# One more VectorE memset among the constants of a decode kernel: two columns of a scratch tensor that nothing reads

## The chip, the cores and the metric

The kernel runs on one core of a Trainium2 chip. A core has five engines that run their own instruction streams and meet at semaphores: TensorE (PE, with its weight loads shown as PEld), VectorE (DVE), ScalarE (ACT), GpSimd (POOL) and SyncE (SP, which here issues nearly all DMAs). The metric is the device time of one execution in microseconds (us); the time before is the median of 3 runs, 192.17 us (192.02 to 192.25).

## The reference

One token is decoded: x is a row of 512. A first block normalizes it, projects it to 32 query heads of 128, attends with 8 key/value heads (each shared by 4 query heads) over 16384 cached positions, and projects back. A second block normalizes again, mixes and goes through an MLP of 1792 with two residual sums.

```
q = (layernorm(x) @ wq)            # 32 heads x 128
scores = q . k_cache / sqrt(128)   # 16384 positions, 8 key heads of 4 queries each
p = softmax(scores)
o = p . v_cache
h = x + o @ wo
out = h + B(layernorm(h))          # B: LN, w1, gelu, shifts, w2, then LN, w3, gelu, w4
```

The caches hold 8 x 16384 x 128 bf16 values each, 33.6 MB for the keys and as much for the values; with the weights that the kernel reads, 79.17 MB come from HBM in one execution. For a single token the shifts of the second block move their one row out of the sequence, so w1 and w2 do not enter, and the kernel does not load them.

## The kernel before, in words

A small class, Program, takes every operation in program order with the keys that it reads and writes, and works out who must wait for whom. When the program is emitted, an operation gets a semaphore increment only if a later one depends on it (`needed`, lines 73 to 85), and each engine's operations are issued in the order in which they were recorded. There is no planner: the order on an engine is the order of the calls.

SyncE first issues three loads: wq (L321, into the buffer that later holds values), and the two halves of the keys of the first pair of heads (L322, L323). ScalarE issues the load of x (L320).

Meanwhile the prologue runs. VectorE fills mean4 and ident_f (L325, L326), GpSimd makes ident_f the identity (L327), VectorE derives quarter (L332, L333). TensorE spreads x over partitions (L335), and `row_sums`, `variance`, `seeds` and `inverse_root` normalize it on VectorE with a few tiny matmuls; the result is the column tensor xn (L341). Then come the constants, which is where the change stands: nscale (L346), zo and zd (L348, L349), reductions of the identity to row32, maskdd, maskgh, rowgh, rowc (L353 to L361) and two copies into zo and zd (L364). At the same time GpSimd zeroes qb and pt (L350, L351). `scr` is a scratch tensor of 128 x 4; ScalarE writes its first column at L347 and its second at L478, only to have the Exp and Gelu tables loaded in time. Its columns 2 and 3 are not used.

When wq has landed, TensorE projects the queries (L375, reads xn and wq), VectorE transposes them (L379) and spreads them into qb (L385).

The main part is a loop over four pairs of key heads. For each half y of a pair's keys, VectorE transposes the half in eight steps (`transpose_keys`, L394, kt from kb), and TensorE multiplies it with the queries (`scores`, L402, 32 matmuls); then SyncE may load the next pair's keys into that half. `softmax` (L413 to L434) follows, `values` (L441) multiplies with the values, `gather` (L452 to L458) collects, and SyncE loads the next values. The second pair's keys (WHOLE) come in one load of both halves.

After the four pairs come wo (L500), the second normalization, w3 (L523), gelu, w4 (L545), the residual sum (L549) and the store of the row (L551). `spin` issues matmuls whose results are not used.

Of the kernel before, what the change touches and what calls it, by code (L numbers as in the profile page):

```python
# [132 lines left out]
def bass_sequential_preLN__gqa_block_cached__mixer_s_mlp__decode_kernel(  # L133
# [13 lines left out]
    with ExitStack() as ctx:  # L147
# [29 lines left out]
        scr = sb("scr", [128, 4], FP32)  # L177
# [62 lines left out]
        def dve(fn, r=(), w=(), bank=()):  # L240
            return P.op("DVE", fn, r, w, bank)

        def act(fn, r=(), w=(), bank=()):
            return P.op("ACT", fn, r, w, bank)
# [99 lines left out]


        dve(lambda e: e.memset(nscale[:, :], -SCALE), w=["nscale"])  # L346
        act(lambda e: e.activation(scr[0:1, 0:1], mean4[0:1, 0:1], ACTF.Exp), r=["mean4"], w=["scr"])  # L347
        dve(lambda e: e.memset(zo[:, :], 0.0), w=["zo"])  # L348
        dve(lambda e: e.memset(zd[:, :], 0.0), w=["zd"])  # L349
# [235 lines left out]
```

## Time and profile before

| what | us |
|---|---|
| median of 3 runs | 192.17 |
| lowest and highest run | 192.02, 192.25 |
| the profiled execution, its own time | 192.12 |
| its span, first to last instruction | 190.4 |
| TensorE matmul busy | 118.2 (62%) |
| VectorE busy | 115.0 (60%), 176 instructions |
| ScalarE busy, GpSimd busy | 9.0, 7.3 |
| HBM read over the span | 79.17 MB, 416 GB/s |
| mean granted TensorE clock | 0.845 |

The page of the profile has the busy time of each engine, the DMA queues, the chain of work that ended last, and groups of instructions. "The chain" is followed back from the last instruction to what released it, and so on; its shares say what the end hung on. In a timeline a row has the start, the duration, engine, line, operation, output <- input with shapes, a count if several were merged, and in brackets how long the engine was idle before it and what ended that. DMA queues of kind "instruction" fetch the engines' code.

### The profile page before, as it was taken

The page shows a single profiled execution, that of the slowest core. Times are in us where ns is not written, and L with a number is a line of the kernel's source. Part 1 is how long each engine was busy: PE and PEld are TensorE (multiplying, and loading weights), DVE is VectorE, ACT ScalarE, POOL GpSimd, SP SyncE. Part 2 cuts the span into 40 slices and gives each one's busy share as a digit, 9 for nine tenths or more (in the row PEclk, how much of TensorE's full clock was granted, in tenths as well). Part 3 has the DMA queues.
Part 4 walks back from the last instruction along what each step waited for, and adds up shares of the span by engine and source line. Part 5 has one row for each costly group of instructions (what it writes and reads, how often), then busy time and mean ns, then how long its engine had stood idle before and what let it go on. Part 6 is the DMA issues. An engine that isn't in the chain of part 4 may idle for free.

```text
span 190.4 us, 1725 instructions
## 1 busy us (share of the span) xinstructions
PE 118.2 (62%) x725; PEld 44.9 (24%) x725; DVE 115.0 (60%) x176; ACT 9.0 (5%) x15; POOL 7.3 (4%) x16
## 2 busy tenths in 40 slices
PE   0129099793083005999449599943739896588673
PEld 0115034221031001422123232212313222233231
DVE  7754697983402008999350999945159897514172
ACT  3000000002000000000110000001000000500011
POOL 7100000000000000000000000000000000000032
PEclk9999859998559655999855789995887999879998
DMA  6999999999999999997999999988999999989991
GB/s 220 441 441 441 441 441 442 441 441 430 441 441 441 441 441 427 441 441 341 441 441 441 530 441 427 416 365 379 434 420 441 468 444 441 427 380 403 443 389 55
DMA packets 2614, 79.26 MB, mean 416 GB/s; under 512 B 304, under 2 KB 432, under 8 KB 560
## 3 DMA queue, kind: packets, MB, share of 16 engines
q1 hardware_dynamic: 2600, 79.17, 97.0%
q8 instruction: 5, 0.08, 0.2%
q14 instruction: 1, 0.01, 0.0%
q10 hardware_dynamic: 8, 0.00, 0.0%
HBM read 79.17 MB, written 0.00 MB: 416 GB/s over the span
## 4 chain that ended last, share of the span: by engine, by line
DMA 60%; DVE 32%; PE 5%; SPq 1%; issue 1%; ACT 1%; ACTq 0%
DMA kb<-in_A_k_cache_dram 46%; DVE kt L394 29%; DMA kb<-in_B_w_dram 14%; PE O_ps L441 3%; DVE pt L428 1%; SPq L221 1%; DVE mx L413 1%; ACT p_sb L424 1%; DVE od L455 1%; PE s_ps L402 1%; PE mn_ps L545 0%; PE mn_ps L418 0%; PE mn_ps L414 0%; DVE od L452 0%; DVE nm L416 0%
## 5 line engine op out<-in xcount | busy, mean ns | idle before, releaser
L402 PE MATMUL s_ps<-kt,qb 128*128 128x512 bf16 x256 | 69.5, 412 | 25.7 <-DVE kt L394 23.0
L394 DVE STREAM_TRANSPOSE kt<-kb 128x1024 int32<-128x1024 int32 x64 | 72.8, 1205 | 18.0 <-DMA kb<-in_A_k_cache_dram 18.0
L402 PEld LDWEIGHTS s_ps<-kt,qb 128*128 128x128 bf16 x256 | 22.9, 103 | 71.3 <-DVE kt L394 46.4
L441 PE MATMUL O_ps<-vb,pt 128*32 128x512 bf16 x256 | 20.1, 484 | 9.8 <-DMA vb<-in_A_v_cache_dram 5.7
L452 DVE TENSOR_SCALAR od<-O_ps,rowc 128x128 f32<-128x128 f32 x4 | 1.4, 351 | 26.2 <-PE O_ps L441 26.2
L441 PEld LDWEIGHTS O_ps<-vb,pt 128*32 128x32 bf16 x256 | 8.4, 119 | 20.7 <-issue 10.9
L428 DVE STREAM_TRANSPOSE pt<-p_sb 64x1024 bf16<-64x1024 bf16 x8 | 9.9, 1239 | 5.4 <-ACT p_sb L424 5.3
L424 ACT ACTIVATE p_sb<-s_ps,bias 128x1024 bf16<-128x1024 f32 x4 | 4.5, 1114 | 156.8 <-DVE nmh L420 156.8
L258 PE MATMUL O_ps<-kt,qb 128*128 128x512 bf16 x31 | 9.3, 443 | 0.0
L413 DVE TENSOR_REDUCE mx<-s_ps 128x1 f32<-128x1024 f32 x4 | 4.9, 1225 | 4.5 <-PE s_ps L402 4.5
L375 PE MATMUL O_ps<-vb,xn 128*64 128x512 bf16 x16 | 3.6, 632 | 5.6 <-DMA vb<-in_A_wq_dram 5.6
L310 POOL TENSOR_SCALAR st<-st 128x1 f32<-128x1 f32 x1 | 0.2, 243 | 177.8 <-DVE st L295 177.8
L430 PE MATMUL A_ps<-acc,zd 128*128 128x1 f32 x8 | 2.1, 337 | 6.3 <-ACT p_sb L424 6.3
L458 PE MATMUL A_ps<-od,zo 128*128 128x128 f32 x8 | 2.0, 326 | 5.5 <-DVE od L455 5.5
L414 PE MATMUL mn_ps<-ident_f,mx 128*1 128x128 f32 x8 | 1.5, 271 | 5.3 <-DVE mx L413 5.3
L455 DVE SCALAR_TENSOR_TENSOR od<-O_ps,rowc,od 128x128 f32<-128x128 f32 x12 | 4.2, 351 | 0.4
L332 DVE CAST ident<-ident_f 4x4 bf16<-4x4 f32 x1 | 3.8, 3847 | 0.6 <-POOL ident_f L327 0.6
L258 PEld LDWEIGHTS O_ps<-kt,qb 128*128 128x128 bf16 x31 | 3.1, 113 | 4.0 <-issue 2.4
L335 PE MATMUL O_ps<-x,quarter 4*128 4x128 bf16 x1 | 0.3, 282 | 5.8 <-DVE quarter L333 5.8
L379 DVE STREAM_TRANSPOSE qcol<-O_ps 128x256 f32<-128x256 f32 x4 | 1.6, 428 | 3.6 <-PE O_ps L375 3.6
L430 PEld LDWEIGHTS A_ps<-acc,zd 128*128 128x128 f32 x8 | 1.8, 280 | 6.6 <-ACT p_sb L424 6.6
L500 PE MATMUL O_ps<-kb,o_b 128*32 128x512 bf16 x32 | 2.1, 381 | 1.7 <-DMA kb<-in_A_wo_dram 1.7
(81 smaller groups left out, 48.1 us busy)
## 6 DMA issues: line engine op xcount, KB each, us to landing
kb<-in_A_k_cache_dram SPq DMA_DIRECT2D x6, 4096.0 KB, 23.2
vb<-in_A_wq_dram SPq DMA_DIRECT2D x1, 4096.0 KB, 12.1
kb<-in_A_wo_dram SPq DMA_DIRECT2D x1, 3072.0 KB, 27.2
kb<-in_B_w_dram SPq DMA_DIRECT2D x1, 1792.0 KB, 24.2
kb<-in_B_w_dram SPq DMA_DIRECT2D x1, 1280.0 KB, 27.0
kb<-in_A_wo_dram SPq DMA_DIRECT2D x1, 1024.0 KB, 29.3
kb<-in_B_w_dram SPq DMA_DIRECT2D x1, 384.0 KB, 27.5
kb<-in_B_w_dram SPq DMA_DIRECT2D x1, 128.0 KB, 27.4
```

The costliest lines, as they stand in the source:

```text
L258: pe(lambda e: e.matmul(O_ps[out][:, :], qb[:, 0, 0, 0:128], kt[:, 0:512], start=True, stop=True), r=["qb", ("kt", 0)], w=[("O", out)], ba ...
L332: dve(lambda e: e.tensor_copy(ident[:, :], ident_f[0:4, 0:4]), r=["ident_f"], w=["ident"])
L375: pe(lambda e, row=row, k=k, g=g, at=at: e.matmul(row[64 * g:64 * g + 64, :], copies(xn[:, k:k + 1], 64), wq_sb[:, at:at + REP * DH], star ...
L394: dve(lambda e, view=view: e.transpose(view(kt), view(kb[y])), r=[("r", y, n) for n in range(RPARTS)], w=[("kt", t)])
L402: pe(lambda e, n=n, c=c: e.matmul(s_ps[:, y, :], qb[:, n, j, QPAD - 4 * c:QW - 4 * c], ktv[:, n // 2, n % 2, :, 8 * c:8 * c + 8, :], start ...
L413: dve(lambda e: e.tensor_reduce(mx[:, :], s_all, AX.X, ALU.max), r=[("s", 0), ("s", 1)], w=["mx"], **both)
L424: act(lambda e: e.activation(p_sb[:, :], s_all, ACTF.Exp, bias=bias[:, 0:1], scale=float(SCALE), accum_out=acc[:, :]), r=[("s", 0), ("s", ...
L428: dve(lambda e, g=g: e.transpose(pt[64 * g:64 * g + 64, :, :, g, :], p_sb[64 * g:64 * g + 64, :]), r=["p"], w=["pt"])
L430: pe(lambda e: e.matmul(A_ps[:, 128:129], zd[:, 96 - 32 * j:224 - 32 * j], acc[:, :], start=(j == 0), stop=(j == PAIRS - 1), skip_group_ch ...
L441: pe(lambda e, q=q, ct=ct, xl=xl, ch=ch: e.matmul(O_ps[j % 2][32 * ct:32 * ct + 32, :], pt[:, xl, ch, :, :].rearrange("p g u -> p (g u)"), ...
L455: dve(lambda e, block=block, c=c: e.scalar_tensor_tensor(od[:, :], block, rowc[:, c:c + 1], od[:, :], ALU.mult, ALU.add), r=[key, "rowc", ...
L500: pe(lambda e, r_=r_, q=q: e.matmul(O_ps[0][32 * q:32 * q + 32, :], copies(o_b[:, r_:r_ + 1], 32), wo_sb[:, r_ * D:(r_ + 1) * D], start=(r ...
```

## The change

One call is added between the memset of nscale and ScalarE's first activation. It writes zeros to columns 2 and 3 of scr on all 128 partitions under a key of its own, "scr2", that no other operation names.

```diff
         dve(lambda e: e.memset(nscale[:, :], -SCALE), w=["nscale"])
+        dve(lambda e: e.memset(scr[:, 2:4], 0.0), w=["scr2"])
         act(lambda e: e.activation(scr[0:1, 0:1], mean4[0:1, 0:1], ACTF.Exp), r=["mean4"], w=["scr"])
         dve(lambda e: e.memset(zo[:, :], 0.0), w=["zo"])
         dve(lambda e: e.memset(zd[:, :], 0.0), w=["zd"])
```

## The prediction

> **What bounds the kernel now.** I read the share of the chain of waits first, then the chain in order of time, then the instructions of the stretch where the change stands, then what the vector engine waits for there, and last the DMA queues. The page's queues (packets, MB, share of the 16 DMA engines' time) and the engines' shares of the chain that ended last:
>
> ```profile
> q1 hardware_dynamic: 2600, 79.17, 97.0%
> q8 instruction: 5, 0.08, 0.2%
> q14 instruction: 1, 0.01, 0.0%
> ...
> DMA 60%; DVE 32%; PE 5%; SPq 1%; issue 1%; ACT 1%; ACTq 0%
> ```
>
> The kernel is bound by its loads: 79.17 MB on one queue whose packets fill 97.0% of the 16 DMA engines' time, and 60% of the chain. VectorE has 32% of the chain, but the chain in order of time says where that share lies:
>
> ```profile
> 1.62 31.52 DMA kb<-in_A_k_cache_dram
> 33.13 0.02 issue
> 33.16 9.14 DVE kt L394 x8
> 42.30 0.02 SPq L101
> 42.32 0.03 issue
> 42.35 29.97 DMA kb<-in_A_k_cache_dram
> 72.32 0.02 issue
> 72.35 18.15 DVE kt L394 x16
> ```
>
> The first 33.13 us of the chain hold no instruction of VectorE at all: the keys' load, issued by 1.62 us, ends that stretch. VectorE enters the chain at 33.16, with the transposes of the second half of the keys. The change stands at about 10.65 us. The timeline of that stretch:
>
> ```profile
> 1.69 3.85 DVE L332 CAST ident<-ident_f 4x4 bf16<-4x4 f32 x1 [0.57 <-POOL ident_f L327]
> ...
> 3.72 1.80 POOL L351 MEMSET pt<- 128x2048 bf16 x1
> ...
> 10.49 0.17 DVE L346 MEMSET nscale<- 1x128 f32 x1
> 10.65 0.24 DVE L348 MEMSET zo<- 128x224 f32 x1
> 10.89 0.24 DVE L349 MEMSET zd<- 128x224 f32 x1
> 11.07 0.23 DVE L353 TENSOR_REDUCE row<-ident_f 128x32 f32<-128x128 f32 x1
> ...
> 12.10 0.18 DVE L364 COPY zd<-maskgh 128x32 f32<-128x32 f32 x1
> ...
> 14.96 0.78 DVE L379 STREAM_TRANSPOSE qcol<-O_ps 128x256 f32<-128x256 f32 x2 [2.68 <-PE O_ps L375]
> ```
>
> The constants run back to back from 10.49 to 12.28; then VectorE stands still for 2.68 us until the query projection delivers. Further on in the same engine's timeline:
>
> ```profile
> 22.62 9.13 DVE L394 STREAM_TRANSPOSE kt<-kb 128x1024 int32<-128x1024 int32 x8 [1.49 <-DMA kb<-in_A_k_cache_dram]
> 33.16 9.13 DVE L394 STREAM_TRANSPOSE kt<-kb 128x1024 int32<-128x1024 int32 x8 [1.41 <-DMA kb<-in_A_k_cache_dram]
> ```
>
> Twice more VectorE is ahead of its data, by 1.49 us and by 1.41 us, before it first matters for the end.
>
> **The change part by part.** It removes nothing and moves nothing in the order of the other engines. It adds one instruction on VectorE, between nscale at L346 and zo at L348, and one instruction to that engine's code.
>
> The instruction's own time. No memset of 128x2 stands in the trace on VectorE. The nearest rows from above are zo and zd, 128x224, 0.24 us each, and 0.24 us from zo's start to zd's; nscale, 1x128, has 0.17 us and 0.16 us to the next start. The nearest row from below is on another engine: the four memsets of 128x1 at the start of GpSimd's timeline begin 0.03 us apart (0.24, 0.27, 0.29, 0.32 us). So the slot is between 0.03 and 0.24 us. I take 0.16, the step from nscale's start, because it is the memset with the fewest elements in a partition on the engine concerned. A gain from the slot itself is excluded: an instruction added in a row that is back to back cannot bring the others forward.
>
> What lies beside it. The constants end at 12.28 + 0.16 = 12.44 us instead of 12.28. The next VectorE instruction starts at 14.96, released by TensorE, so 2.52 of the 2.68 us are left: cost nothing. Does TensorE wait for the constants? The table of waits names the last copy, zd at L364, as what ended 5.6 us of idle weight-load time before L375, and the DMA of wq as what ended 5.6 us of the matmuls' idle time there. L375 reads only xn and the wq buffer in the code, and xn was done by 10.25 + 0.29 = 10.54 us, ahead of the change. So I take the DMA as the releaser: zd is merely the latest event of that engine. Even with the worse reading, zd ended at 12.28 and the weight load began at 12.97, which leaves 0.69 us for a shift of at most 0.24. Nothing that the constants make is wanted early: maskgh first at L420 (45.87 us), rowc at L452 (58.25 us).
>
> If that cover were gone, 0.16 to 0.24 us would go to the projection, then into the 1.49 us that VectorE waits for the first keys at 22.62, and still not to the end. SyncE's next issue after the first three loads is the values at 19.51 us, behind the projection; a delay of 0.24 us there would leave the queue full, since the keys it already holds land only at 33.13.
>
> Semaphores. The helper gives an increment only to an operation on which another depends. Nobody reads or writes the new key afterwards, so the instruction neither waits nor signals, and every other wait keeps its number. Nothing is queued behind a new wait, on any engine. The scratch tensor keeps its size, so no buffer moves. No DMA is added.
>
> The code. VectorE's stream is one instruction longer, so a fetch of code bound to a place in that stream comes one instruction earlier. The page shows six such packets: five on q8 (0.08 MB together) and one on q14 (0.01 MB). Narrow windows of the DMA view place the q14 packet between 30 and 31 us, with 1.9% of 16 engines in 1 us, that is 0.30 us of one engine; a q8 packet between 43 and 45 us has 3.4% of 2 us, that is 1.09 us. If the q14 packet is VectorE's, it moves forward by one transpose, 9.13 / 8 = 1.14 us, within the same wait for the keys. VectorE's eight transposes around it run with no gap that the timeline shows (9.13 us, as in the undisturbed group at 33.16), so today a fetch stalls nothing; I set zero. The two ends: +1.09 us if the move exposes a whole fetch on the chain, and -1.09 us if a fetch that now holds up the last packets of a load on the chain gets out of its way.
>
> The Trainium skill, "Runtime: NRT & Kernel Launch", section "Instruction fetch mechanics", says that code comes in 16 KiB blocks fetched while the current one executes, and that crossing a block's boundary is mostly hidden. By that rule the sum is the same zero. This trace agrees on the hiding, and on the block for q8 (0.08 MB in 5 packets), not for q14, whose packet is 0.01 MB.
>
> The sum. 0.16 us of VectorE, all inside 2.68 us of idle time; +0.00 on the path. The profiled execution has 192.12 us, of which 190.4 is the span and 1.72 lies around it. I expect 192.12 + 0.00, and as the median of the runs shown is 192.17, 0.05 above the profiled one, I give 192.17.
>
> **The rivals.** A measurement of this kernel can tell about 0.2%, 0.38 us, from no change; the three runs shown lie within 0.23 us.
>
> Slower, by a code fetch. The longer stream moves the place where VectorE needs new code to a point on the chain: the transposes at 33.16 to 42.30, 72.35 to 90.50, or those of the two later pairs. Price 0.30 us (the q14 packet) to 1.09 us (a q8 packet), giving 192.47 to 193.26; it decides from 0.38 us on, and only beyond 33.16, since before that 1.41 us of waiting for the keys absorbs it. For it: six fetches do happen, five beside work on which the end depends. Against it: none of VectorE's groups of eight transposes shows a gap, and five of six fetches are on a queue that shows up again and again while TensorE works through its far longer stream (1450 of 1725 instructions).
>
> Slower, by a collision with GpSimd. The 4x4 cast at L332 took 3.85 us where the copy after it took 0.21, and it ended at 5.54 when GpSimd's memset of pt ended (3.72 + 1.80 = 5.52). A small VectorE instruction can thus cost 3.64 us too much. Price of the same for the new memset: 3.64 - 2.68 = 0.96 us late at the projection, taken up by the 1.49 us before the keys, so 192.17 again; it decides only if the delay passes 2.68 + 1.49 = 4.17 us plus 0.38. Against it: GpSimd has no instruction between 5.52 us and its steps of the second normalization after 183 us, so there is nothing to collide with at 10.65. The Trainium skill, "SBUF — State Buffer", calls the port pair that these two engines share an exclusive lock, held for the whole instruction, which fits the cast's 3.85 us; by that rule too the memset is free here.
>
> Faster, by a code fetch out of the way. The fetch that shares the DMA engines with the keys' load ending at 33.13 comes elsewhere, and the load lands earlier. Price 0.30 us for the q14 packet, 191.87, under the bound; with a large one 1.09 us, 191.08. Against it: moved by 1.14 us the packet is still within the same load.
>
> No change because nothing is there: the dead memset is dropped in the build. That ends at 192.17 too.
>
> **How the numbers follow.** No effect (hidden or dropped, the collision included): 0.72. A fetch exposed on the chain: 0.20, of which about 0.16 passes the bound. A fetch out of the way: 0.08; and some 0.04 more on this side is for a shift between two builds of the same work that I can't name, so faster 0.11, same 0.72, slower 0.17. The likeliest case gives 192.17. Its own range is that of the runs shown with 0.1 us around it, 191.9 to 192.4. The range asked for takes in the small form of the faster case (191.87) and over half of the fetch's prices: 191.85 to 192.80; what is left out are the large fetches on either side, about 0.15.
>
> **What would show it.** Right: a memset on scr of about 0.1 to 0.2 us at 10.65, zo at about 10.8, the last constant ending by 12.5; the wait before L379 down from 2.68 to about 2.5 with its start still at 14.96; the keys' landings at 33.13 and 72.32 unmoved; the chain's lines with the same shares. If the q14 packet is VectorE's, it stands near 29.4 instead of 30.5. Wrong: the first group of eight transposes over 9.13 us or a gap inside a group (a fetch), the keys landing other than at 33.13, a start of L375 other than 12.97, or a code packet more than the six.

## The result and the profile after

The change made the kernel faster by a little: 191.75 us median (22 runs, 191.53 to 191.98) against 192.07 us for the kernel before (22 runs beside them, 191.84 to 193.44), a ratio of 0.9978 with a 95% interval of 0.9971 to 0.9986. The time predicted was 192.17 with a range from 191.85, so the median lies 0.10 us below the range, and on the side that had a chance of 0.11.

The first thing to look at is where the 0.32 us are. The profiled execution after has 191.53 us and a span of 190.2, so 1.3 us lie around the span; before it was 192.12 and 190.4, so 1.7. Over all runs that list a span, the medians are:

| | time | span | time less span, median | its range |
|---|---|---|---|---|
| before (31 runs of a later call) | 192.11 | 190.4 | 1.69 | 1.63 to 1.75 |
| after (22 runs) | 191.75 | 190.4 | 1.34 | 1.28 to 1.39 |

The span did not change. What lies around it became 0.35 us shorter, and the two ranges do not touch. So the gain isn't in any work that the page shows. The page after says the same: in its part on the queues and in the chain's shares there is nothing new.

```profile
q1 hardware_dynamic: 2600, 79.17, 97.1%
q8 instruction: 5, 0.08, 0.2%
q14 instruction: 1, 0.01, 0.0%
...
DMA 61%; DVE 31%; PE 4%; issue 1%; SPq 1%; ACT 1%; ACTq 0%
```

The timeline of the stretch with the change (start, duration, engine, line, operation):

```profile
10.50 0.17 DVE L346 MEMSET nscale<- 1x128 f32 x1
10.62 0.06 DVE L347 MEMSET scr<- 128x2 f32 x1
10.67 0.24 DVE L349 MEMSET zo<- 128x224 f32 x1
...
12.12 0.17 DVE L365 COPY zd<-maskgh 128x32 f32<-128x32 f32 x1
...
15.18 0.78 DVE L380 STREAM_TRANSPOSE qcol<-O_ps 128x256 f32<-128x256 f32 x2 [2.88 <-PE O_ps L376]
```

The memset is there and takes 0.06 us. From nscale's start to zo's it is 0.17 us where it was 0.16, and the last constant ends at 12.29 instead of 12.28. All of this lies in front of 2.88 us of idle time. The projection started 0.22 us later because wq landed 0.22 us later in this execution (the run below with the memset late in the program, whose prologue is the old one, has the projection's first weights at 13.14 instead of 12.97 too). The chain in order of time shows how little that matters:

```profile
1.63 31.27 DMA kb<-in_A_k_cache_dram
32.90 0.03 issue
32.92 9.14 DVE kt L395 x8
42.06 0.02 SPq L101
42.08 0.03 issue
42.11 30.19 DMA kb<-in_A_k_cache_dram
72.30 0.02 issue
72.32 18.16 DVE kt L395 x16
```

The second half of the keys landed at 32.90 instead of 33.13, but the second pair's keys landed at 72.30 instead of 72.32: the early gain is lost within one load.

What comes after the span is not on the page, but the trace records every update of a semaphore, with its time. After the last DMA of the kernel a first barrier ends (its last update of semaphore 2 is at 190.70 us before, 190.50 after), then the other semaphores are reset in five rows side by side, read here as one row for each engine, and then semaphore 2 is updated nine times more, in the last barrier: five updates up a row of engines and four back, as the records are read here; they do not name the engines. (The Trainium skill, "Runtime: NRT & Kernel Launch", section "Semaphores 0–2 are reserved", gives semaphore 2 to the sync barrier, which fits this record.) These are the nine in us from the span's start, worked out from the records of both traces:

```
before  191.515 191.550 191.588 191.631 191.655 | 192.123 192.161 192.195 192.242
after   191.293 191.327 191.365 191.409 191.432 | 191.533 191.571 191.605 191.652
```

From one update to the next it is 0.02 to 0.05 us, and at the turn of the row it is 0.10 us after the change, but 0.47 us before it. One engine answered 0.37 us late at the turn in the kernel before. That is nearly all of the 0.40 us by which the time less the span of these two executions differs; the other 0.03 us lie ahead of the barrier. In the barrier that opens the kernel the turn takes 0.11 us in both traces.

### The profile page after: what moved, and what is told of

Same layout as the page of the kernel before. It is cut to its first block, busy times and chain, and to the rows that moved or that the text cites. A ratio compares the mean times of both kernels' runs of the same rounds, so it can differ in the third digit from the quotient of the medians.

```text
span 190.2 us, 1723 instructions
## 1 busy us (share of the span) xinstructions
PE 116.9 (61%) x722; PEld 43.7 (23%) x725; DVE 115.0 (60%) x177; ACT 9.0 (5%) x15; POOL 7.4 (4%) x16
## 4 chain that ended last, share of the span: by engine, by line
DMA 61%; DVE 31%; PE 4%; issue 1%; SPq 1%; ACT 1%; ACTq 0%
DMA kb<-in_A_k_cache_dram 46%; DVE kt L395 28%; DMA kb<-in_B_w_dram 14%; PE O_ps L442 3%; DVE pt L429 1%; SPq L221 1%; DVE mx L414 1%; ACT p_sb L425 1%; DVE od L456 1%; PE s_ps L403 1%; PE mn_ps L546 0%; PE mn_ps L419 0%; PE mn_ps L415 0%; DVE od L453 0%; DVE nm L417 0%
## 5 line engine op out<-in xcount | busy, mean ns | idle before, releaser
L403 PEld LDWEIGHTS s_ps<-kt,qb 128*128 128x128 bf16 x256 | 22.3, 102 | 72.7 <-DVE kt L395 49.4
L376 PEld LDWEIGHTS O_ps<-vb,xn 128*64 128x64 bf16 x16 | 1.5, 168 | 7.1 <-DVE zd L365 5.8
```

Of the source, the lines that this page charges most:

```text
L376: pe(lambda e, row=row, k=k, g=g, at=at: e.matmul(row[64 * g:64 * g + 64, :], copies(xn[:, k:k + 1], 64), wq_sb[:, at:at + REP * DH], star ...
L403: pe(lambda e, n=n, c=c: e.matmul(s_ps[:, y, :], qb[:, n, j, QPAD - 4 * c:QW - 4 * c], ktv[:, n // 2, n % 2, :, 8 * c:8 * c + 8, :], start ...
```

## The experiments

The theory to be tested (A): VectorE is the engine that is late. Somewhere in its stream it has to wait for its code, in the kernel before this falls on its answer in the last barrier, and one instruction more moves it by one. From the run with four more on the theory is more exact: one late step of about 0.35 us at each change from a block of code to the next, 128 or more instructions apart. The rivals: any newly built program gets rid of the delay by luck (B); the gain lies in the span after all (C); the pattern repeats every few instructions (A2). "Around the span" is always the time less the span, median over the runs.

**Two memsets.** In place of the one memset, two of one column each.

```diff
+        dve(lambda e: e.memset(scr[:, 2:3], 0.0), w=["scr2"])
+        dve(lambda e: e.memset(scr[:, 3:4], 0.0), w=["scr3"])
```

> Two memsets of one column each after nscale instead of the change's one. In the two profiled runs the span differs by 0.2 us (190.4 and 190.2) and what lies around it by 0.39 (1.72 and 1.33). Theory A (VectorE's code position: one instruction more moves what VectorE executes after its last kernel instruction, in the closing barrier, off a place where it waits for code): around the span about 1.33, time about 191.75, unless two instructions reach the next such place. Rival B (any newly built program that differs from the one before gets rid of the 0.39 us by luck): also 1.33. Rival C (the gain lies inside the span, in the loads): around the span 1.72, and the span shorter by 0.3.

Measured: 191.83 us, ratio 0.9990 (0.9980 to 0.9999), span 190.4, around the span 1.44 (1.41 to 1.46), where A had expected 1.33. The turn of the barrier is free (0.10 us), but the fourth update comes 0.15 us after the third instead of 0.04, a delay of 0.11 that stands in the sum. C falls, since the span is as before. B is not told apart yet, but 0.11 late at another update speaks for a delay that moves forward with the count.

**The memset on GpSimd.**

```diff
         pool(lambda e: e.memset(pt[:, :, :, :, :], 0.0), w=["pt"])
+        pool(lambda e: e.memset(scr[:, 2:4], 0.0), w=["scr2"])
```

> The same memset of two columns, given to GpSimd behind its memset of pt instead of to VectorE, whose code is then as before. Theory A: around the span 1.72 as before, time about 192.07. Rival B: 1.33, time about 191.75. Rival C: around the span 1.72, the span undecided.

Measured: 192.13 us, ratio 1.0010 (0.9988 to 1.0032), around the span 1.70, and the turn of the barrier takes 0.47 us. A new program with the same VectorE code keeps the delay: B falls.

**The memset late in the program.** The change's line, moved in front of o_m.

```diff
+        dve(lambda e: e.memset(scr[:, 2:4], 0.0), w=["scr2"])
         dve(lambda e: e.scalar_tensor_tensor(o_m[:, :, :], A_ps[:, 0:128].rearrange("p (d r) -> p d r", d=4),
```

> The change's memset at another place of VectorE's program: ahead of o_m, at about 175 us, in the 0.58 us that VectorE waits there. Theory A counts instructions, not where they stand: around the span 1.33, time about 191.75. Rival B: 1.33 too. Rival C (the prologue's timing makes the gain): nothing of the prologue moves, so 1.72 around the span and 192.07.

Measured: 191.67 us, ratio 0.9980 (0.9971 to 0.9989), around the span 1.34, the turn 0.11 us. The timeline shows it at its new place, in front of o_m:

```profile
174.66 0.06 DVE L490 MEMSET scr<- 128x2 f32 x1
175.29 0.35 DVE L491 SCALAR_TENSOR_TENSOR o_m<-A_ps,den,maskdd 128x128 f32<-128x128 f32 x1 [0.57 <-PE A_ps L458]
```

The same gain without touching the prologue: where the instruction stands makes no difference, only that VectorE has one more.

**One instruction fewer.**

```diff
-        zo = sb("zo", [128, 224], FP32)
-        zd = sb("zd", [128, 224], FP32)
+        zz = sb("zz", [128, 448], FP32)
+        zo, zd = zz[:, 0:224], zz[:, 224:448]
...
-        dve(lambda e: e.memset(zo[:, :], 0.0), w=["zo"])
-        dve(lambda e: e.memset(zd[:, :], 0.0), w=["zd"])
+        dve(lambda e: e.memset(zz[:, :], 0.0), w=["zo", "zd"])
```

> One VectorE instruction fewer than before: zo and zd are halves of one tensor, zeroed by one memset. Theory A: the place moves the other way; the late arrival of 0.39 us stays or grows if the place lies behind (around the span 1.72 or more), or goes (1.33) if just one position is bad. Rival B: 1.33. Rival C: 1.72 around the span.

Measured: 192.18 us, ratio 1.0005 (0.9995 to 1.0014), around the span 1.65. The barrier's nine updates show no delay (turn 0.10 us), but the profiled execution's time, laid off from the span's start, ends 0.23 us after the last of them, where it ends 0.12 us before it in the kernels before and after. The delay has moved the other way, behind the barrier, and still counts. The expectation had left A both ways open, so the time alone does not test it; the place of the delay does.

**Four and eight more, with a tensor of their own.** The memsets write a tensor `pad` allocated behind scr; with 8 for 4 in the second.

```diff
         scr = sb("scr", [128, 4], FP32)
+        pad = sb("pad", [128, 4], FP32)
...
         dve(lambda e: e.memset(nscale[:, :], -SCALE), w=["nscale"])
+        for c in range(4):
+            dve(lambda e, c=c: e.memset(pad[:, c:c + 1], 0.0), w=[("pad", c)])
```

> Four memsets of one column behind nscale. So far, around the span (time less span): 1.65 with one VectorE instruction fewer, 1.69 with as many as before, 1.34 with one more, 1.44 with two more. Theory A1 (one late step of about 0.35 at a fixed far position of VectorE's stream, 128 or more instructions apart from the next one; it now falls among the resets of semaphores ahead of the last barrier, where other engines are later): 1.33. Rival A2 (code is delivered in lines of four instructions, so the pattern has a period of four): 1.69 as before.

> Eight memsets of one column behind nscale. Theory A1: 1.33 around the span, as with four. Rival A2, in lines of four or of eight instructions: 1.69.

Measured with four: 190.98 us (3 runs), ratio 0.9950 (0.9928 to 0.9973), span 189.5, around it 1.49 (1.43 to 1.58). With eight: 191.08 (3 runs), 0.9947 (0.9924 to 0.9969), span 189.8, around it 1.30. A2 falls: neither has 1.69. For eight A holds; for four A's detail was wrong, 1.49 where 1.33 was expected. And the span is 0.6 to 0.9 us shorter, which no theory had foreseen: a second matter, taken up below.

The records of the run with four also show where its delay went. Of the five rows of resets between the two closing barriers, the one of semaphores 156 to 206 begins 0.51 us after the first barrier's last update; in the thirteen other traces it begins 0.02 to 0.03 us after it. The other four rows begin where they always do. VectorE's is the only program that got longer here, and traces with the same buffers but another count do not show it, so the row is taken to be VectorE's, with a delay of 0.49 us ahead of it. Most of that is hidden: the row ends at 0.81 us instead of about 0.34, another row ends at 0.56, and the last barrier begins at 0.81, where it begins at 0.79 to 0.82 in the other traces.

**Two and three fewer.** Besides zo and zd in one memset, nscale is filled by GpSimd, and for three mean4 too.

```diff
-        dve(lambda e: e.memset(nscale[:, :], -SCALE), w=["nscale"])
         pool(lambda e: e.memset(pt[:, :, :, :, :], 0.0), w=["pt"])
+        pool(lambda e: e.memset(nscale[:, :], -SCALE), w=["nscale"])
...
-        dve(lambda e: e.memset(mean4[:, :], -1.0 / (32 * D)), w=["mean4"])
+        pool(lambda e: e.memset(mean4[:, :], -1.0 / (32 * D)), w=["mean4"])
```

> Two VectorE instructions fewer: zo and zd in one memset, nscale zeroed by GpSimd instead. Theory A1: the late step falls one instruction later than with one fewer, on VectorE's last steps behind the last barrier; 1.65 if these still count, about 1.33 if it is past the last one. Rival A2 with lines of four: this is the same place as two more, 1.44.

> Three VectorE instructions fewer: mean4 also filled by GpSimd, ahead of its first operation. The span may be some tenths longer, since GpSimd's start is in the way of the identity matrix, but the prologue has slack. Around the span, theory A1: 1.33 (past the last step that counts) or 1.65 if not yet; never between. Rival A2 with lines of four: as with one more, 1.34.

Measured with two fewer: 192.01 us, ratio 0.9996 (0.9985 to 1.0008), around the span 1.55. With three fewer: 191.70 us, ratio 0.9981 (0.9970 to 0.9992), around the span 1.30. With three fewer the delay is gone; with two it is partly behind the end (the time ends 0.11 us after the last update), between the two values that A had named.

**Only the unused bytes.** No instruction is added; the tensor alone moves the key and value buffers by 32 bytes.

```diff
         scr = sb("scr", [128, 4], FP32)
+        pad = sb("pad", [128, 8], FP32)
```

> No instruction added: only an unused tensor of 32 bytes per partition behind scr, as the runs with four and eight memsets had it; it puts the key and value buffers at 48128 and 113664 bytes instead of 48096 and 113632 (multiples of 64 instead of 32 above one). Those two runs had spans of 189.4 to 189.8 us against 190.4. Theory L (the layout makes the shorter span, the instructions do not): span 189.6, around the span 1.69 as before, time about 191.3. Rival (the instructions make it): span 190.4, time 192.1.

Measured: 191.38 us, ratio 0.9966 (0.9954 to 0.9979), span 189.7, around it 1.70 with the turn at 0.47 us. So the shorter span belongs to the layout, and the delay in the barrier does not care for it. The span's difference lies in the loads. The chains of this kernel and of the kernel before go the same way, and their four loads add up to 113.93 us with the 32 bytes and to 114.73 before. The last two of them, the kernel before first:

```profile
124.44 25.75 DMA kb<-in_A_k_cache_dram
160.27 27.49 DMA kb<-in_B_w_dram
```

and with the 32 bytes:

```profile
124.56 25.17 DMA kb<-in_A_k_cache_dram
159.81 27.17 DMA kb<-in_B_w_dram
```

The records of q1's packets agree: those of 65536 bytes take 2.418 us in the median instead of 2.421, and all of them together 184.1 us on the average of the 16 DMA engines instead of 184.7 (184.5 to 184.8 in the ten traces with the old addresses, 184.1 to 184.4 in the four with the new). The page's GB/s in 40 slices can't show this: a steady slice holds the same 2.10 MB in both, so its 442 instead of 441 says only that a slice of the shorter span is shorter.

**Eight more without moving a buffer.** The tensor is allocated behind all others.

```diff
         kt = sb("kt", [128, 128 * DH], BF16)
+        pad = sb("pad", [128, 8], FP32)
...
+        for c in range(8):
+            dve(lambda e, c=c: e.memset(pad[:, c:c + 1], 0.0), w=[("pad", c)])
```

> Eight memsets of one column behind nscale, but their target is allocated behind all other tensors, so that no buffer moves. Theory L: span 190.4, around the span 1.30 as with eight before, time about 191.7, and the small packet of VectorE's code again inside the span, near 188 to 189 us. Rival (the instructions shorten the span): span 189.6, time 190.9.

Measured: 191.76 us, ratio 0.9980 (0.9971 to 0.9990), span 190.4, around it 1.36, the turn 0.10 us. The two effects are apart. The DMA view of 184 to 190 us of this kernel has a packet of code, which the same window of the kernels before and after lacks:

```profile
q1 hardware_dynamic: 346, 0.92, 39.1%
q14 instruction: 1, 0.01, 0.5%
```

The records place it at 188.34 us, and the one that stood at 30.51 before at 23.36. So eight more VectorE instructions draw the packets on q14 forward: they are VectorE's code, at least in part. The run with four more has such a packet at 190.68 us, behind its span.

**128 more.** As a packet has 8192 bytes, 128 instructions would be one packet if each has 64 bytes. They run where VectorE waits for the second pair's keys.

```diff
             gather(j)
+            if j == 0:
+                for c in range(128):
+                    dve(lambda e, c=c: e.memset(pad[:, c:c + 1], 0.0), w=[("pad", c)])
             if j < PAIRS - 1:
```

> 128 memsets of one column in the 12.6 us that VectorE waits before the second pair's keys, target behind all other tensors: 128 x about 0.03 = some 4 us, hidden, span 190.4. The code packets on that queue have 8192 bytes; if an instruction has 64 bytes, 128 instructions are one packet. Theory A1 with that block: the place in the closing steps is the same as before's, around the span 1.69, and one packet more inside the span. Rival (blocks of 256, or no period at all): another value, most likely 1.30.

Measured: 192.30 us, ratio 1.0012 (1.0001 to 1.0022), around the span 1.69, and the turn of the barrier takes 0.45 us again, nearly as in the kernel before. The span is 190.6, 0.2 longer than expected, for which no cause was looked for. The page has one code packet more on q14 (the record has it at 68.95 us):

```profile
q14 instruction: 2, 0.02, 0.0%
```

And here the step itself can be seen, since it falls among the added memsets. VectorE's timeline:

```profile
59.83 1.12 DVE L456 SCALAR_TENSOR_TENSOR od<-O_ps,rowc,od 128x128 f32<-128x128 f32 x3
60.90 2.64 DVE L479 MEMSET pad<- 128x1 f32 x115
63.86 0.40 DVE L479 MEMSET pad<- 128x1 f32 x13 [0.33 <-issue]
```

115 memsets follow one another, nearly all in steps of 0.01 to 0.03 us and never over 0.06. Then VectorE stands still, waits for nothing that the profile shows, and goes on 0.39 us after the last start: 0.36 more than the usual step, about what the turn of the barrier had too much (0.37). Nowhere else in the 128 is there such a gap, so the period is not 16, 32 or 64.

The memset behind the gap is the 187th of the 304 VectorE instructions that the page counts, and the 192nd of the 312 that the trace records, with the waits and the drain that the page leaves out. The kernel before has 184 of these, and then come the closing steps. If they go on in the same stream, one place each, the late step falls on the eighth of them; with 128 more it is again the eighth (192 + 128 = 320, eight past 312). One instruction fewer makes it the ninth, two more the sixth, four more the fourth. That is the order in which the delay was found, from the end backwards: behind the last update, at the turn (the kernel before), at the fourth update, ahead of the resets.

What VectorE does in these 0.36 us is not shown. No packet of code moves during the gap at 63.5 to 63.9 us, the additional one comes 5 us later, and in the kernel before the last packet of code is at 181.03 us. So the delay goes with the count of instructions, but it is not the time of a packet that arrives just then.

**Both gains together.** Three VectorE instructions fewer, and the 32 unused bytes.

> Both gains: three VectorE instructions fewer, as in the run of that name, and the 32 unused bytes. Around the span 1.30, span 189.6, time about 190.9, 0.6% under before, if the two are independent and theory L holds; 191.7 if the layout does nothing.

Measured: 191.03 us (4 runs), ratio 0.9945 (0.9930 to 0.9960), span 189.7, around it 1.35 (1.33 to 1.47), the turn 0.10 us. It beats both kernels; the run with four memsets in its own tensor (0.9950) and the one with eight (0.9947) can't be told from it. Giving two constants to GpSimd also adds two waits to TensorE's program, so this is not three instructions alone.

All counts in one view, around the span, relative to the kernel before:

| VectorE instructions | -3 | -2 | -1 | 0 | +1 | +2 | +4 | +8 | +128 |
|---|---|---|---|---|---|---|---|---|---|
| us around the span | 1.30 | 1.55 | 1.65 | 1.69 | 1.34 | 1.44 | 1.49 | 1.30 to 1.36 | 1.69 |

## Why the prediction was wrong

**The instruction's slot.** Forecast 0.16 us between the bounds 0.03 and 0.24; the step from nscale to zo grew by 0.01, and among the 128 memsets the steps were mostly 0.01 to 0.03. The far row, GpSimd's 128x1 memsets, was the right one, and nscale was not. Nothing hung on it.

**Its cover.** Right: the wait before the query transposes was longer than the slot, the projection waited for wq, and the span is 190.4 in both. Nothing on another engine waited for the new instruction. Two of the prediction's signs of being wrong did appear, the keys at 32.90 and a later start of the projection, but neither moved the end.

**The sum.** This is the step that failed. It read "192.12 + 0.00" and took the 1.72 us around the span over as a constant. They were not: 0.37 us of them were a delay of VectorE in the closing barrier, and with one more instruction the delay is gone from there. The forecast looked for effects of the longer code only inside the span, on the chain.

**The code.** The mechanism was named in part, a block of code that comes at another place, and the wrong places were looked at. The rival "faster, by a code fetch out of the way" put it into the keys' load, with 0.30 us as its small price; the gain of 0.35 has nothing to do with a load. That the price lies near the gain is chance. The price was bounded by the time that a packet takes on a DMA engine (0.30 to 1.09 us); the late step was measured at 0.37 in the barrier and at 0.36 among the memsets. The forecast that the q14 packet would move from 30.5 to about 29.4 was wrong too: it came at 30.28 with one instruction more, at 31.52 with the late memset, at 23.36 with eight. How the request for a packet follows the count is open.

**The hiding.** VectorE's packets are of 8192 bytes here, and a period of 128 instructions fits the runs; the late step was hidden where VectorE had slack, and cost 0.37 us in the barrier and 0.36 us among short instructions. The prediction had weighed the Trainium skill, "Runtime: NRT & Kernel Launch", section "Instruction fetch mechanics": blocks of 16 KiB, the crossing mostly hidden. The measurement decides.

**The range.** It missed by 0.10 us. Its lower end was the small form of the faster rival, 191.87; 192.17 less the measured 0.35 would have been 191.82, and the kernel before had 192.07 in the runs beside the changed kernel, another 0.10 lower than the median that the forecast started from.

Open: why one more shows nothing of the delay, two and four more 0.10 and 0.15 us of it, and two fewer 0.2. In the run with four the third and fourth update of the barrier are 0.09 us apart instead of 0.04, and the rest lies behind the last update. Which closing steps these are wasn't tried.

## What to carry to other kernels

Put the time less the span beside every comparison: when it moves and the span doesn't, look at the closing barrier before looking for a cause in the kernel's work. On this kernel the number of instructions on one engine decided where a delay of 0.36 us fell, and a single instruction that does nothing was worth 0.2%; so a difference of that size between two versions says little about their ideas until the same count has been tried with a dummy. And an edit that adds a tensor also moves the buffers behind it, so allocate dummies last.

## What was not expected of the hardware

At one place in VectorE's stream a step costs about 0.36 us, seen twice (0.47 against 0.10 us at the turn of the barrier, 0.39 against 0.03 among 128 memsets), and once 0.49 us ahead of its resets. A period of 128 instructions fits these runs: with 128 more the delay was back at the turn, and one more packet of 8192 bytes came.

Moving the key and value buffers by 32 bytes, from 48096 and 113632 to 48128 and 113664, shortened the span from 190.4 to 189.7 us, ratio 0.9966 (0.9954 to 0.9979). The new addresses are multiples of 64 bytes and the old ones are not; whether that is the reason, or which of the moved buffers matters, wasn't tried.
